# Wave 1 of a fused attention and MLP kernel: a third group of half-block products in place of four half-wave items, and another order of GpSimd's casts

## The chip, the cores and the metric

The kernel runs on one core of a Trainium2 chip. Its engines are TensorE (PE, with its weight loads shown as PEld), VectorE (DVE), ScalarE (ACT), GpSimd (POOL) and SyncE (SP, which issues most DMAs). Each engine works through its own instructions in the order of the program; semaphores hold an instruction until what it needs is there. The metric is the device time of one execution in microseconds (us).

## The reference

Linear attention with a decay for each head, block by block, and then an MLP on all 3072 tokens (4 batches of 768 positions, 8 heads of 64 make 512 columns; the hidden width is 2048):

```python
for b in range(nb):                       # blocks of 64 positions
    intra = np.einsum('bhic,bhjc->bhij', qb, kb) * Dmask[None]
    intra = np.einsum('bhij,bhjd->bhid', intra, vb)
    inter = np.einsum('bhid,bhde->bhie', qb * lam_pow[None], kv_state)
    out[:, :, sl] = intra + inter
    kv_state = lam_block[None, :, None, None] * kv_state + np.einsum('bhsd,bhse->bhde', kb * rev_pow[None], vb)
x = out.transpose(0, 2, 1, 3).reshape(B * S, H * D)
h = x @ w_in                              # 512 -> 2048
g = h * (1.0 / (1.0 + np.exp(-1.702 * h)))
return g @ w_out                          # 2048 -> 512
```

## The kernel before, in words

The tokens are worked in six waves of 512. Waves 0 and 1 take the first 256 positions of two batches each; waves 2 to 5 take 128 positions of all four batches. A wave is: load q, k and v (SP), scale and cast q and k to bf16 (`do_cast`, on GpSimd or VectorE), turn them so that the head dimension lies on the partitions (`turn_pe` on TensorE, or `turn_dma`, a transposing DMA that SP issues), attention, and the two products of the MLP. The attention of wave 1 goes by its two batches: `start(1, c)` makes the scores, which VectorE masks (`sm`, line 267), and `end(1, c)` multiplies them by v (`d_out`, line 316) and has ScalarE copy the result from PSUM into `xT`, the wave's x (line 221).

**Half-block products.** The MLP's products save an eighth of the multiplications by the seven-product scheme for 2 x 2 blocks. For the first product the two block rows are the two halves of the wave's tokens (256 each), the inner blocks the two halves of the 512 columns of x, and the two block columns are pairs of 128-wide blocks of the hidden width; four such blocks are a group (`GROUPS`). The factors of the seven products are blocks of x or the four sums `x_s` (`x_sums`, line 529, VectorE: s3, s1, s2 and s4 in that order, the last two depending on the one before), and blocks of `w_in` or sums of them (`in_sums`, line 520). In `in_product` (line 544 for the matmuls) each product is four matmuls of 128 x 256. Products 1 and 2 need only the first token half and no sum; 7 needs s3, 6 needs s2, 5 needs s1, 3 needs s4, and 4 needs the second token half. Products 1, 6, 5 and 3 pile up in one PSUM bank (X) one after the other, with a copy or an addition out of the bank after each; 2 has the bank Q, and 7 and 4 share V.

In the list of steps (`STEPS`, read by `one_step`) a small letter is the group's place and the digit the product: `a7v` is product 7 of the wave's first group, with `v` for "copied out by VectorE" (line 218), otherwise 1, 6 and 7 are copied out by ScalarE (line 221). The results of 2, 5 and 4 are added on VectorE to such a copy (`h_sb`, line 552). A capital letter is the GELU of a finished quarter on ScalarE (`A2`, line 563). `P10` is product 1 of the MLP's second product for the first 128 tokens of a half (line 461), `gl3` a sum of its factors (`g_s`, line 441, VectorE), where `l` and `h` are the lower and the upper half of the hidden width; `S0` to `S3` are the scores of the next wave (line 335), `M` and `m` their masks.

**Half-wave items.** `mlp1_half(w, c, fc)` computes two hidden blocks for one token half in the plain way: eight matmuls of 128 x 256 (line 414) into one bank and one GELU (line 416). Wave 1 has eight of them for hidden blocks 0 to 3 and 5 to 8, and seven-product groups only for the other eight blocks (`GR` gives group numbers for each wave).

**Order around the change.** All engines' work is written out by hand in program order (`manual_schedule`), and each engine keeps that order. Between `end(1, 0)` and the list for wave 1 the program has: a half-wave item, product 3 of wave 0 (`P31`), `start(1, 1)`, two items, `end(1, 1)`, an item, `x_sums(1)`, and four items of the second token half. GpSimd's casts of wave 2 stand among them in the order k, q, k, q (first half of the batches, then the second), each followed by its transposing DMA on SP. `gate_pool` is a one-element copy on GpSimd, used to make it wait until something is written; waves 2 to 5 have one behind `x_s` (step `G`).

Of the kernel before, what the change touches and what calls it, by code (L numbers as in the profile page):

```python
# [25 lines left out]
def kernel(  # L26
# [13 lines left out]
    nc = tc.nc  # L40
# [7 lines left out]
    G = W // P  # L48
# [14 lines left out]
    NW = S // P  # L63
# [9 lines left out]
    HF = 2  # L73
# [18 lines left out]
    def load(w, nms="kqv"):  # L92
        src = {"k": k, "q": q, "v": v}
        if w < ND:
            for c in range(HF):
                for nm in nms:
                    if w or c == 0 or nm != "v":
                        load_one(w, c, nm, src[nm])
        else:
            for nm in nms:  # L100
                for c in range(HF):
                    load_one(w, c, nm, src[nm])
# [140 lines left out]
    def turn_dma(w, c, nm):  # L243
        y = work.tile([P, 2 * NP, P], bf16, tag=f"{nm}T{c}", bufs={"k": 1, "q": 2}[nm], name=f"{nm}T")
        nc.sync.dma_start_transpose(out=y, in_=cast[w, c, nm].rearrange("p b c -> p (b c)"))
        trans[w, c, nm] = y
# [159 lines left out]
    def mlp1_half(w, c, fc):  # L406
        if w not in g_of:
            g_of[w] = gp.tile([P, FFC, W], bf16, tag="g", name="g_sb")
        cols = slice(c * W // 2, (c + 1) * W // 2)
        h = acc("ps_h", shape=[P, 2, W // 2], tag="mm")  # L410
        for u in range(2):
            j, i = w_in_of[fc + u]
            for kc in range(KC):
                nc.tensor.matmul(h[:, u, :], w_in_sb[j][:, kc, i * P : (i + 1) * P], xT[w][:, kc, cols],  # L414
                                 start=(kc == 0), stop=(kc == KC - 1))
        nc.scalar.activation(g_of[w][:, fc : fc + 2, cols], h, GELU)
# [13 lines left out]
    def token_half(w, i, kh):  # L430
        return g_of[w].rearrange("p (m two) (i t) -> p two i m t", two=2, i=2)[:, kh, i]
# [16 lines left out]
    def product(w, n, ts, ms=range(FFC // 2)):  # L448
        last = w == NW - 1
        key = ts[0] if last else 0  # L450
        if n == 1 and (last or ts[0] == 0) and ms[0] == 0:
            for c in "QVX":
                blocks[w, c, key] = acc(f"ps_{c}", shape=[P, 2, 256], tag="a" if last and ts[0] else "mm")
        bank = blocks[w, CHAIN[n], key]
        sums, raw = half_sum.get(w, [None] * 4), [[token_half(w, i, kh) for kh in range(2)] for i in range(2)]
        x = {1: raw[0][0], 2: raw[0][1], 4: raw[1][1], 5: sums[0], 6: sums[1], 7: sums[2], 3: sums[3]}[n]
        for t in ts:
            for m in ms:
                y = {1: (0, 0), 2: (1, 0), 3: (1, 1)}.get(n)
                y = w_half(m, *y) if y else TS[{4: 3, 5: 0, 6: 1, 7: 2}[n]][:, m]  # L460
                nc.tensor.matmul(bank[:, t], x[:, m, t * P : (t + 1) * P], y,  # L461
                                 start=(n in (1, 2, 7) and t == ts[0] * last and m == 0),
                                 stop=(m == FFC // 2 - 1), skip_group_check=True)
        if (last or ts[-1] == 1) and ms[-1] == FFC // 2 - 1:
            t = slice(ts[0], ts[0] + 1) if last else slice(0, 2)
            if n == 2 and w < NW - 1:
                c11[w] = partial(after_product, w, n, bank, t)
            else:
                after_product(w, n, bank, t)
# [24 lines left out]
                out=out.rearrange("(b s) d -> s b d", s=S)[w * P : (w + 1) * P, 2 * i + t.start : 2 * i + t.stop, cols],  # L494
                in_=o[:, t])

    GR = {w: (1, 2, 0, 3) if w > 1 else (0, 3) for w in range(1, NW)}
    TAGS = {w: ("aQXV", "mXVQ", "aQXV", "aXVQ") if w > 1 else ("aQXV", "aXVQ") for w in range(1, NW)}
    HALVES = (0, 2, 5, 7)
    GROUPS = (((4, 13), (14, 15)), ((0, 2), (1, 3)), ((6, 5), (8, 7)), ((10, 9), (12, 11)))  # L500
    USED = sorted({g for w in range(NW) for g in GR.get(w, ())})
    TI = {g: [const.tile([P, KC // 2, 2, P], bf16, name=f"w_in_t{g}{n}") for n in range(1, 5)] for g in USED}
# [22 lines left out]
    def x_sums(w):  # L525
        s1, s2, s3, s4 = x_sum[w] = [xp.tile([P, 2, 256], bf16, tag=f"xs{n}", bufs=1, name="x_s") for n in range(4)]
        a11, a12, a21, a22 = (x_half(w, i, kh) for i in range(2) for kh in range(2))
        for o, x, y, f in ((s3, a11, a21, SUB), (s1, a21, a22, ADD), (s2, s1, a11, SUB), (s4, a12, s2, SUB)):
            nc.vector.tensor_tensor(o, x, y, op=f)  # L529
# [35 lines left out]
    def one_step(w, s):  # L565
        if s[0] == "+":
            w, s = w + 1, s[1:]
        x, a = w + 1, s[1:]
        if s[0] == "f":
            mlp1(w, int(a))  # L570
        elif s[0] in "abcd":
            k = "abcd".index(s[0])
            in_product(w, GR[w][k], int(s[1]), TAGS[w][k], dve_copy if s[2:] == "v" else act_copy)
        elif s[0] in "ABCD":
            in_gelu(w, GR[w]["ABCD".index(s[0])], int(a))
        elif s[0] == "P":
            product(w, int(s[1]), (int(s[2]),))
        elif s[0] == "p":
            product(w, int(s[1]), (0, 1), {"a": range(4), "b": range(4, 6), "l": range(6), "h": range(6, 8)}[s[2]])
        elif s[0] == "W":  # L580
            weight_sums(int(a[0]), tuple(int(i) - 1 for i in a[1:]))
        elif s[0] == "I":
            in_sums(int(a))
        elif s[0] in "kq":
            do_cast(x, int(a), s[0], nc.vector)
        elif s[0] in "KQ":
            do_cast(x, int(a), s[0].lower(), nc.gpsimd)
        elif s[0] == "t":
            turn_dma(x, int(s[2]), s[1])
        elif s[0] == "v":  # L590
            cast_v(x, int(s[1]), ((act_copy, dve_copy)[s[2:] == "v"],))
        elif s[0] == "S":
            n_scores(x, int(a))
        elif s[0] == "M":
            n_masks(x, int(a))
        elif s[0] == "m":
            n_masks(x, int(a), True)
        elif s[0] == "R":
            n_rest(x)
        elif s[0] == "o":  # L600
            c11.pop(w)()
        elif s[0] == "X":
            x_sums(x)
        elif s[0] == "G":
            gate_pool(x_sum[w][3][0:1, 0, 0:1])
        elif s[0] == "g":
            m0, m1 = {"l": (0, 4), "h": (4, 8)}[s[1]]
            g_sums(w, m0, m1, tuple(int(c) - 1 for c in s[2:]))
        elif s[0] == "L":
            load(w + (1 if a == "w" else 2), "kq" if a == "k" else "v")  # L610
        else:
            raise ValueError(s)

    STEPS = {
# [24 lines left out]
    with tc.manual_schedule():  # L639
# [55 lines left out]
        def start(w, c):  # L695
            if c == 0:
                d_one(w, c)
                d_keep(w, c)
            for pp in range(2):
                d_scores(w, c, pp)  # L700
            d_even(w, c, ("mm", "a")[c])

        def end(w, c):
            oa, oz = d_out(w, c)
            t = acc("ps_kv", shape=[P, NP, D]) if w else states[w, c]
            if w == 0:
                nc.scalar.copy(seen, oz[:, 3, P - 1 : P])
            d_state(w, c, t, Z)
            if w == 0:
                d_inter(w, c, oz, 0, False)  # L710
            if w and c == 0:
                d_one(w, 1)
            d_x(w, c, 0, oa, act_copy)
            d_x(w, c, 1, oz, act_copy if w and c else dve_copy)
            if w:
                nc.vector.tensor_tensor(kv_sb[0][:, 2 * w + c], kept[w, c], t, op=ADD)
            else:
                nc.scalar.copy(kv_sb[0][:, 2 * w + c], t)
            if w and c == 0:
                d_keep(w, 1)  # L720

        def steps(w, names):
            for s in names.split():
                one_step(w, s)
# [23 lines left out]
        end(1, 0)  # L748
        steps(0, "P30 I2")
        turn_pe(1, 1, "q", act_copy)  # L750
        halves = [(c, fc) for c in range(HF) for fc in HALVES]
        for i, (c, fc) in enumerate(halves):
            if i == 1:
                steps(0, "P31")
                start(1, 1)
            if i == 3:
                end(1, 1)
            if i == 4:
                x_sums(1)
            mlp1_half(1, c, fc)  # L760
            if i in (1, 2, 3, 4):
                nm = "kq"[(i - 1) % 2]
                do_cast(2, (i - 1) // 2, nm, nc.gpsimd)
                turn_dma(2, (i - 1) // 2, nm)
            if i == 6:
                load(2, "v")
        steps(1, STEPS[1])
        for w in range(ND, NW):
            steps(w, STEPS[w])
# [30 lines left out]
```

## Time and profile before

| | |
|---|---|
| median of 3 runs | 192.86 us (192.72 to 193.34) |
| the profiled execution | 192.84 us; its span, first to last instruction, 191.1 us |
| PE busy | 184.6 us (97% of the span) |
| DVE busy | 156.3 us (82%) |
| ACT busy | 129.6 us (68%) |
| POOL busy | 53.7 us (28%) |
| TensorE clock granted | 1.00 |

The profile has one execution. In a timeline row the first number is the start of the first instruction, the second how long the merged instructions lasted, then engine, line, operation, the tile written and the tiles read, shapes, and in brackets how long the engine stood idle and what ended that. The start of a matmul is its issue; matmuls overlap, so a row of four 128 x 256 matmuls that lasts 0.60 us takes 0.44 us of the engine until the next row starts. In the chain of waits the rows are laid end to end.

### The profile page before, as it was taken

To read this page: it belongs to the slowest core of one execution; us is meant where nothing else is said; L and a number is where in the kernel's file an instruction comes from. 1 tells how busy PE (TensorE), PEld (TensorE's weight loads), DVE (VectorE), ACT (ScalarE), POOL (GpSimd) and SP (SyncE) were. 2 spreads that over 40 slices of the span, in tenths; PEclk is the share of its full clock that TensorE was granted. 3 is DMA by queue.
4 is the path that set the end of the run, shared out by engine and by line. 5 is a ranking of instruction groups with operands and counts; after the bars stand their busy time and mean duration, and the time that the engine had idled before them with its cause. 6 is when DMAs were issued, how large, how long until landed. Compare 5 with 4: busy or idle time off the path is not lost.

```text
span 191.1 us, 5544 instructions
## 1 busy us (share of the span) xinstructions
PE 184.6 (97%) x2297; PEld 152.2 (80%) x2297; DVE 156.3 (82%) x292; ACT 129.6 (68%) x242; POOL 53.7 (28%) x76
## 2 busy tenths in 40 slices
PE   7979999999999999999999999999999999999993
PEld 2557646888888888888888888888888888888882
DVE  1796699979978799879799879799789797888950
ACT  4948665257666986388896288885488876597611
POOL 5499000076495000195000294000492000000000
PEclk9999999999999999999999999999999999999999
DMA  4999999999997997868999555899565903300113
GB/s 144 313 290 197 204 200 209 321 310 229 215 241 178 214 247 165 207 163 139 208 243 216 187 153 127 197 241 230 175 152 122 209 4 113 110 3 0 54 59 110
DMA packets 89599, 33.91 MB, mean 177 GB/s; under 512 B 67430, under 2 KB 89446, under 8 KB 89574
## 3 DMA queue, kind: packets, MB, share of 16 engines
q1 hardware_dynamic: 84676, 28.84, 60.1%
q0 software_dynamic: 4896, 4.72, 14.5%
q8 instruction: 18, 0.29, 0.6%
q14 instruction: 7, 0.06, 0.1%
q10 hardware_dynamic: 2, 0.00, 0.0%
HBM read 27.26 MB, written 6.29 MB: 176 GB/s over the span
## 4 chain that ended last, share of the span: by engine, by line
PE 73%; DMA 11%; DVE 8%; POOL 2%; ACT 2%; issue 1%; SPq 0%; ACTq 0%
PE ps_X L461 19%; PE ps_hX L544 16%; PE ps_V L461 9%; PE ps_hV L544 8%; PE ps_Q L461 5%; DMA w_in<-in_moe_w_in_dram 5%; PE ps_hQ L544 4%; DVE w_in_t L520 3%; DMA kf<-in_k_dram 3%; DMA vf<-in_v_dram 3%; PE ps_h L414 2%; PE ps_s L335 2%; PE ps_o L390 2%; PE ps_fill L147 2%; POOL ks L202 1%; DVE sm L267 1%
## 5 line engine op out<-in xcount | busy, mean ns | idle before, releaser
L461 PEld LDWEIGHTS <-g_s 128*128 128x128 bf16 x384 | 37.0, 98 | 5.0
L563 ACT ACTIVATE g_sb<-h_sb 128x512 bf16<-128x512 f32 x54 | 32.6, 631 | 1.2 <-DVE h_sb L552 1.2
L544 PEld LDWEIGHTS <-w_in_t 128*128 128x128 bf16 x288 | 28.1, 98 | 3.4
L461 PEld LDWEIGHTS <-g_sb 128*128 128x128 bf16 x288 | 27.4, 98 | 4.1
L221 ACT COPY part<-ps_hX 128x512 f32<-128x512 f32 x32 | 18.3, 586 | 11.5 <-PE ps_hX L544 11.5
L461 PE MATMUL ps_X<-w_out_t,g_s 128*128 128x256 bf16 x192 | 23.1, 273 | 0.0
L544 PEld LDWEIGHTS <-w_in 128*128 128x128 bf16 x216 | 21.1, 98 | 2.5
L544 PE MATMUL ps_hX<-x_s,w_in_t 128*128 128x256 bf16 x144 | 21.6, 272 | 0.0
L441 DVE TENSOR_TENSOR g_s<-g_sb 128x1024 bf16<-128x1024 bf16 x24 | 16.3, 687 | 5.9 <-ACT g_sb L563 5.6
L634 POOL CAST behind_q<-x_s 1x1 f32<-1x1 bf16 x3 | 0.5, 174 | 60.3 <-DVE x_s L529 60.3
L209 POOL TENSOR_TENSOR qs<-qf,q_pow 128x512 bf16<-128x512 f32 x16 | 16.6, 1063 | 2.9 <-DMA qf<-in_q_dram 2.9
L209 POOL TENSOR_TENSOR ks<-kf,k_pow 128x512 bf16<-128x512 f32 x16 | 16.8, 1075 | 1.8 <-DMA kf<-in_k_dram 1.8
L474 ACT COPY part<-ps_X 128x512 f32<-128x512 f32 (+1 forms) x14 | 7.3, 522 | 13.0 <-PE ps_X L461 13.0
L218 DVE COPY part<-ps_hV 128x512 f32<-128x512 f32 x18 | 12.4, 688 | 3.7 <-PE ps_hV L544 3.7
L552 DVE TENSOR_TENSOR h_sb<-part,ps_hX 128x512 f32<-128x512 f32 x18 | 12.3, 681 | 2.7 <-PE ps_hX L544 2.7
L552 DVE TENSOR_TENSOR h_sb<-part,ps_hV 128x512 f32<-128x512 f32 x18 | 12.3, 684 | 1.0 <-PE ps_hV L544 1.0
L461 PE MATMUL ps_X<-w_out,g_sb 128*128 128x256 bf16 x96 | 12.6, 273 | 0.0
L461 PE MATMUL ps_Q<-w_out,g_sb 128*128 128x256 bf16 x96 | 12.5, 273 | 0.0
L552 DVE TENSOR_TENSOR h_sb<-part,ps_hQ 128x512 f32<-128x512 f32 x18 | 12.2, 679 | 0.0
L461 PE MATMUL ps_V<-w_out_t,g_sb 128*128 128x256 bf16 x96 | 12.0, 273 | 0.0
L563 ACT ACTIVATE g_sb<-ps_hX 128x512 bf16<-128x512 f32 x18 | 10.6, 588 | 1.8 <-PE ps_hX L544 1.8
L461 PE MATMUL ps_V<-w_out_t,g_s 128*128 128x256 bf16 x96 | 11.6, 273 | 0.0
(111 smaller groups left out, 362.3 us busy)
## 6 DMA issues: line engine op xcount, KB each, us to landing
kf<-in_k_dram SPq DMA_DIRECT2D x10, 512.0 KB, 6.4
qf<-in_q_dram SPq DMA_DIRECT2D x10, 512.0 KB, 7.2
vf<-in_v_dram SPq DMA_DIRECT2D x10, 512.0 KB, 6.0
out_dram<-o_sb SPq DMA_DIRECT2D x24, 128.0 KB, 2.4
out_dram<-o_sb SPq DMA_DIRECT2D x12, 256.0 KB, 2.7
w_out<-in_moe_w_out_dram POOLq DMA_DIRECT2D x4, 512.0 KB, 14.1
kf<-in_k_dram SPq DMA_DIRECT2D x4, 256.0 KB, 3.1
qf<-in_q_dram SPq DMA_DIRECT2D x4, 256.0 KB, 5.2
```

The lines of the kernel that those rows point to most:

```text
L147: nc.tensor.matmul(fill_ps[0], zero[:, 0:P], zero, start=True, stop=True)
L209: eng.tensor_tensor(x.rearrange("p b (r i j d) -> p j (b r) i d", i=2, j=2, d=D)[:, j], f.rearrange("p h (a d) -> p (h a) d", a=2).rearran ...
L218: nc.vector.tensor_copy(out, in_)
L221: nc.scalar.copy(out, in_)
L335: nc.tensor.matmul(s2[h][:, b, :], kT[hs, (b % 2) * NP + p, :], qT[hs, (b % 2) * NP + p, :], start=True, stop=True)
L441: nc.vector.tensor_tensor(o, x, y, op=f)
L461: nc.tensor.matmul(bank[:, t], x[:, m, t * P : (t + 1) * P], y, start=(n in (1, 2, 7) and t == ts[0] * last and m == 0), stop=(m == FFC // ...
L474: nc.scalar.copy(part[w, n, t.start][:, t], bank[:, t])
L520: nc.vector.tensor_tensor(o, x, y, op=SUB)
L544: nc.tensor.matmul(bank[:, u], z[:, kc], y[:, kc], start=(n in (1, 2, 7) and u + kc == 0), stop=(kc == 1), skip_group_check=True)
L552: nc.vector.tensor_tensor(h, h_part[w, g, {2: 1, 5: 7, 4: 6}[n]], bank, op=ADD)
L563: nc.scalar.activation(g_of[w][:, a : b + 1 : b - a, 256 * i : 256 * i + 256], bank, GELU)
```

## The change

Wave 1 gets a third group (blocks 0 to 3) computed by seven products, ahead of the other two, and four of the eight half-wave items go (blocks 0 to 3); the two items of the second token half move into the list of steps. GpSimd casts both k of wave 2, then waits for the last of the sums of x (`G`), then casts both q; the transposing DMAs on SP follow that order. The first group takes its banks from the pool of three (`mXVQ`), the other two from the pool of five.

```diff
-    GR = {w: (1, 2, 0, 3) if w > 1 else (0, 3) for w in range(1, NW)}
-    TAGS = {w: ("aQXV", "mXVQ", "aQXV", "aXVQ") if w > 1 else ("aQXV", "aXVQ") for w in range(1, NW)}
-    HALVES = (0, 2, 5, 7)
+    GR = {w: (1, 2, 0, 3) if w > 1 else (1, 0, 3) for w in range(1, NW)}
+    TAGS = {w: ("aQXV", "mXVQ", "aQXV", "aXVQ") if w > 1 else ("mXVQ", "aQXV", "aXVQ") for w in range(1, NW)}
+    HALVES = (5, 7)
...
+        elif s[0] == "h":
+            mlp1_half(w, 1, int(a))
...
     STEPS = {
-        1: ("a1 a7v a2 a6 b1 b7v A2 a5 b2 b6 B2 a4 a3 b5 b4 A5 P10 A4 b3 gl3 B4 B5 P11 gh3 S0 S1 M0 P20 m1 "
+        1: ("b2 a7v a6 b7v A2 a5 b6 a4 A5 a3 c1 A4 B2 b5 c7v c2 c6 B5 b3 b4 h5 C2 c5 B4 h7 c4 P10 c3 C5 P11 gl3 "
+            "C4 gh3 S0 S1 M0 P20 m1 "
             "Lk gl1 P70 P71 gl2 P21 v0 gh12 S2 S3 M2 m3 v1 o P40 P41 P60 gl4 gh4 P61 R P50 P51 +a1 X +a2 P30 "
             "P31 "),
...
-        halves = [(c, fc) for c in range(HF) for fc in HALVES]
-        for i, (c, fc) in enumerate(halves):
-            if i == 1:
-                steps(0, "P31")
-                start(1, 1)
-            if i == 3:
-                end(1, 1)
-            if i == 4:
-                x_sums(1)
-            mlp1_half(1, c, fc)
-            if i in (1, 2, 3, 4):
-                nm = "kq"[(i - 1) % 2]
-                do_cast(2, (i - 1) // 2, nm, nc.gpsimd)
-                turn_dma(2, (i - 1) // 2, nm)
-            if i == 6:
-                load(2, "v")
+        mlp1_half(1, 0, HALVES[0])
+        steps(0, "P31")
+        start(1, 1)
+        for c in range(HF):
+            do_cast(2, c, "k", nc.gpsimd)
+            turn_dma(2, c, "k")
+        mlp1_half(1, 0, HALVES[1])
+        steps(1, "a1 a2")
+        end(1, 1)
+        steps(1, "b1")
+        x_sums(1)
+        steps(1, "G")
+        for c in range(HF):
+            do_cast(2, c, "q", nc.gpsimd)
+            turn_dma(2, c, "q")
+        load(2, "v")
         steps(1, STEPS[1])
```

## The prediction

> **What bounds the kernel now.** I read the page first, for the engines' shares:
>
> ```profile
> PE 184.6 (97%) x2297; PEld 152.2 (80%) x2297; DVE 156.3 (82%) x292; ACT 129.6 (68%) x242; POOL 53.7 (28%) x76
> ```
>
> TensorE is busy nearly throughout, but a share over the span doesn't tell what happens in the stage that is changed. So next comes the chain of waits around wave 1:
>
> ```profile
> 47.52 2.80 DVE w_in_t L520 x3
> 50.32 2.41 DVE sm L267 x4
> ...
> 53.44 4.47 PE ps_h L414 x40
> 57.91 0.44 PE ps_hX L544 x4
> 58.35 0.44 PE ps_hV L544 x4
> ...
> 64.91 0.87 PE ps_X L461 x8
> 65.78 0.56 PE ps_s L335 x16
> ```
>
> Up to 52.7 VectorE carries it (sums of weights, then the four masks). From 53.44 to the end of the program it is TensorE without a hole: five half-wave items (40 matmuls), then the products. So whatever takes work off TensorE after 53.4 is worth just that work, and every wait that appears there is paid in full: no later idle time of TensorE can take it back. Third, VectorE's timeline, and GpSimd's beside it:
>
> ```profile
> 54.21 2.29 DVE L529 TENSOR_TENSOR x_s<-xT 128x512 bf16<-128x512 bf16 x2 [0.24 <-ACT xT L221]
> 56.54 1.15 DVE L529 TENSOR_TENSOR x_s<-x_s,xT 128x512 bf16<-128x512 bf16 x1
> 57.73 1.15 DVE L529 TENSOR_TENSOR x_s<-xT,x_s 128x512 bf16<-128x512 bf16 x1
> 58.83 0.69 DVE L218 COPY part<-ps_hV 128x512 f32<-128x512 f32 x1
> 59.43 0.68 DVE L552 TENSOR_TENSOR h_sb<-part,ps_hQ 128x512 f32<-128x512 f32 x1
> ...
> 66.10 0.69 DVE L441 TENSOR_TENSOR g_s<-g_sb 128x1024 bf16<-128x1024 bf16 x1 [0.72 <-ACT g_sb L563]
> ...
> 78.68 0.75 DVE L529 TENSOR_TENSOR x_s<-xT 128x512 bf16<-128x512 bf16 x2
> 79.47 0.42 DVE L529 TENSOR_TENSOR x_s<-x_s,xT 128x512 bf16<-128x512 bf16 x1
> 79.92 0.42 DVE L529 TENSOR_TENSOR x_s<-xT,x_s 128x512 bf16<-128x512 bf16 x1
> ```
>
> ```profile
> 52.99 2.05 POOL L209 TENSOR_TENSOR qs<-qf,q_pow 128x512 bf16<-128x512 f32 x2 [2.94 <-DMA qf<-in_q_dram]
> 55.00 2.42 POOL L209 TENSOR_TENSOR ks<-kf,k_pow 128x512 bf16<-128x512 f32 x2
> ```
>
> The reader should see three things. The four sums of x take 4.67 us in wave 1 (54.21 to 58.88), beside GpSimd's casts, and 1.66 us in wave 2 (78.68 to 80.34), where GpSimd stands still. In wave 1 that slowness is free, because TensorE's 40 matmuls, begun at 53.37, last until 57.75. And the sums can't begin before 54.2: ScalarE's copies of x release them.
>
> **The change, part by part.** All is summed against the profiled execution, 192.84 us (span 191.1 and 1.7 around it); the median of the runs is 192.86.
>
> TensorE's work: four items of eight matmuls (32) become seven products of four (28). A matmul of 128 x 256 takes 0.109 us (the 40), a product 0.436. Gain: 4 x 0.109 = 0.44 us, all on the path.
>
> Before 53.4: between the scores of `start(1, 1)` and `end(1, 1)` there stood two items, 16 matmuls; now an item, a1 and a2, also 16. The bank of a2 is the one that P31's result leaves at 50.22 (ScalarE's copy at 49.64, 0.58 long); a2's turn is at 51.53. So `end(1, 1)` and the copies of x stay where they are, the sums again start at 54.21, and the change is worth nothing here. The second k cast now follows the first: it needs a load issued at about 43.8 that takes 6.4 us (median of the page), so it runs from 50.2 to 52.3 or, at 1.23 us each, 52.7. It lies beside the masks at 50.25. Four masks beside GpSimd's casts at 43.07 took 2.48 us and 2.47 here without: nothing for it. And it is over before 54.21, so I take wave 2's pace for the sums: s3 ready at 54.63, s2 at 55.42, s4 at 55.87. That takes 3.0 us of work off VectorE, which was hidden.
>
> The cover is what goes. Behind `end(1, 1)` stood five items, 4.37 us, that need no sum; now only b1 and b2 stand there, until 54.25. Following TensorE's new order (b1, b2, a7, a6, b7, a5, b6, a4, a3), with three latencies: 0.05 us from a VectorE result to the matmul (mask ends 52.72, matmul 52.77); 0.64 us from a product's start to the start of the copy or addition that empties its bank (58.19 to 58.83); 0.60 us between VectorE's copies and additions in a row (58.83 to 59.43):
>
> a7 needs s3: 54.68 instead of 54.25, a wait of 0.43. a6 needs s2: 55.47 instead of 55.12, 0.35. a5 goes into the bank that ScalarE copies after a6: 55.47 + 0.64 + 0.58 + 0.05 = 56.74, and only b7 stands between (until 56.34): 0.40. In waves 2 to 5 two products stand there, just enough. Then b6 and a4 run until 58.05. a3 needs VectorE's addition of a5. After the sums VectorE has b2's addition at 55.80 (1.59 after the sums' start, as at 80.27 in wave 2), the copies of a7 and b7 at 56.40 and 57.00, and that addition at 57.60, ending at 58.28: a3 at 58.33, a wait of 0.28. Two chains, one over ScalarE (58.05) and one over VectorE (58.33), end near each other, so removing one alone would give little back. Sum of waits: 0.43 + 0.35 + 0.40 + 0.28 = 1.46 us.
>
> From a3 on, eleven products, two items and P10 (4.80 + 1.75 + 0.87 us) lead to P11 at 65.75; it was at 64.75 before. I find no wait in between: c6 comes at 60.5 and needs the copy of c1, done at 60.05 on ScalarE; b3 at 60.95 needs an addition done at 60.53; c5, c3 and both items have over half a microsecond.
>
> One more appears behind it. `C4`, a GELU, now stands behind ScalarE's copy of P11, and `gh3` needs it. The copy of P11 starts at 66.97 (P11's end plus 0.2, behind two GELUs 0.5 apart), C4 runs from 67.45 to 68.08, gh3 (0.69) ends at 68.80. P70's fifth matmul needs that; its turn is at 68.60 (P70 follows P11's start by 2.41, as 67.16 did 64.75). Wait: 0.25 us. Before, gh3 ended at 66.79, 0.8 us early. VectorE goes on with the masks at 68.71 instead of 66.71, 2.0 later, and TensorE is 1.25 later; the last masks of wave 2, which ended at 73.42, end at 75.4, and their matmuls, which began at 74.59, want them from 75.8 on. It has caught up when the next sums of x are due. I put nothing for it, and up to 0.3 if the masks slip.
>
> Added evictions: three additions and one copy on VectorE (4 x 0.68 = 2.7 us, less than the 3.0 that the sums give up), two copies of 0.59 on ScalarE, whose 9.9 busy of 12.9 us hold them. They cost nothing apart from the waits named. GpSimd's gate (0.17 us) holds the two q casts until 56.1; behind it on GpSimd there is nothing else before wave 3. Four casts of 1.05 end at 60.3. SP's queue has k's second transposing DMA at 58.0 and q's at 59.4 and 60.7, as it had four at 56.2 to 60.7 before; the load of v behind them stays at 62.0. The last lands near 63.5; S0 wants it at 66.7. Hidden with 3 us to spare, and beyond that each microsecond would cost one.
>
> Sum: -0.44 + 1.46 + 0.25 = +1.27 us, 194.1 us.
>
> **The rivals.** *TensorE is fed in time.* If sums, copies and additions are done when their products' turn comes, only the work counts: 192.84 - 0.44 = 192.4. It speaks for this that VectorE gets 3.0 us back and is idle for 18% of the span. It is decided by a5's addition: a3's turn without waits is 53.37 + 8 x 0.436 = 56.9, so the addition has to end by then, and for no loss by 57.3; I have it at 58.28, and the ScalarE chain alone at 58.05. Chance 0.09.
>
> *The sums stay slow.* Should k's second load land over 1.5 us later, its cast lies beside the sums again. At the rows of wave 1 (4.67 instead of 1.66 us) a3 moves by 3.0 us: 197.1. Against it: the load was issued in the same place, and GpSimd waits for nothing else. Chance 0.05. [...]
>
> *The clock falls.* Four holes in four microseconds might lower the granted clock. Priced at half speed for the eight products after a3, 8 x 0.436 = 3.5 us: 197.6. Against it stands this row of the waits, a hole twice as long as any here, with the granted clock at 1.00 throughout:
>
> ```profile
> PE ps_t L238 <- DVE qs L202: 0.9, 1, 0.9
> ```
>
> Chance 0.02. [...]
>
> **How the numbers follow.** The forecast has 0.82; 0.02 is for what I haven't seen. Its own range: without the wait at P70 and with latencies 0.1 us shorter at the five waits, 193.3; with the sums at their mean of 0.57 us (0.6 more) and another 0.3 for the masks, 195.0. These ends hold about 0.8 of all cases, so they are the range. What can be told from no change is about 0.3%, 0.58 us. Faster by more than that can't come from 0.44 us: 0.02. The same: the first rival and the forecast's low tail, 0.12. Slower: 0.86.
>
> **What would show it.** Right: sums of x near 0.42 us each; TensorE idle before a7, a6, a5 and a3 by 0.3 to 0.4 us each; P11 at about 65.8 and the scores at 66.7; the fifth matmul of P70 waiting for a `g_s` row near 68.8; no other hole behind. Wrong: x_s rows above 1 us, a6 and a3 following without a hole, or a P11 before 65.0.

## The result, and the profile after

The changed kernel takes 194.38 us (median of 20 runs), the kernel before, measured beside it, 193.03 us (median of 20). The ratio, which here as in every experiment leaves out runs more than 1.5% above the fastest of their kernel, is 1.0062, with a 95% interval of 1.0039 to 1.0086. The kernel is slower by 1.2 us, about twice what can be told from no change. The profiled execution took 193.97 us with a span of 192.3 us, 1.13 us more than before. Its trace has no record of the clock, but its 128 x 256 matmuls are issued 0.109 us apart wherever nothing holds them, as before.

The page's line of the engines says next to nothing of it:

```profile
PE 185.4 (96%) x2293; PEld 152.0 (79%) x2293; DVE 154.7 (80%) x296; ACT 130.4 (68%) x244; POOL 53.8 (28%) x77
```

TensorE has four matmuls fewer and 0.8 us more busy time. Half of that lies ahead of the changed stage (50.5 us up to the end of wave 1's attention, 50.1 before). The other half is a matter of reading: a matmul that ends a burst is shown at its full 0.27 us, though the next could follow after 0.109, and five holes bring that five times. What happened stands in the timeline of wave 1 (start, length, engine, line, operation, tiles; in brackets the idle time and its releaser; "..." where rows are left out, among them all weight loads):

```profile
54.08 0.76 DVE L529 TENSOR_TENSOR x_s<-xT 128x512 bf16<-128x512 bf16 x2 [0.31 <-ACT xT L221]
54.55 0.60 PE L544 MATMUL ps_hV<-x_s,w_in_t 128*128 128x256 bf16 x4 [0.27 <-DVE x_s L529]
54.87 0.42 DVE L529 TENSOR_TENSOR x_s<-x_s,xT 128x512 bf16<-128x512 bf16 x1
55.33 0.42 DVE L529 TENSOR_TENSOR x_s<-xT,x_s 128x512 bf16<-128x512 bf16 x1
55.35 0.61 PE L544 MATMUL ps_hX<-x_s,w_in_t 128*128 128x256 bf16 x4 [0.20 <-DVE x_s L529]
55.67 0.68 DVE L552 TENSOR_TENSOR h_sb<-part,ps_hQ 128x512 f32<-128x512 f32 x1
...
56.00 0.59 ACT L221 COPY part<-ps_hX 128x512 f32<-128x512 f32 x1 [1.47 <-PE ps_hX L544]
...
56.27 1.28 DVE L218 COPY part<-ps_hV 128x512 f32<-128x512 f32 x2
...
56.64 1.03 PE L544 MATMUL ps_hX<-x_s,w_in_t 128*128 128x256 bf16 x8 [0.24 <-ACT part L221]
57.47 0.68 DVE L552 TENSOR_TENSOR h_sb<-part,ps_hX 128x512 f32<-128x512 f32 x1
...
58.20 0.60 PE L544 MATMUL ps_hX<-x_s,w_in 128*128 128x256 bf16 x4
...
66.84 0.58 ACT L474 COPY part<-ps_X 128x512 f32<-128x512 f32 x1
...
67.30 0.64 ACT L563 ACTIVATE g_sb<-h_sb 128x512 bf16<-128x512 f32 x1
...
67.98 0.69 DVE L441 TENSOR_TENSOR g_s<-g_sb 128x1024 bf16<-128x1024 bf16 x1 [2.17 <-ACT g_sb L563]
68.03 2.18 PE L461 MATMUL ps_V<-w_out_t,g_s 128*128 128x256 bf16 x16
```

The four sums run at 0.42 us, from 54.08 to 55.75. The matmul rows show a7 at 54.55, a6 at 55.35, a5 at 56.64 and a3 at 58.20, three of them with a releaser in brackets: twice a sum, once ScalarE's copy. The brackets (0.27, 0.20, 0.24) are smaller than what is lost, because a matmul's modelled end lies beyond the issue of the next. The loss is read from issue to issue, less the 0.109 us that a matmul takes of the engine: 0.435 us ahead of a7, 0.366 ahead of a6, 0.400 ahead of a5, 0.256 ahead of a3. The fifth hole hides inside a row: the 16 matmuls of the last line last 2.18 us where they lasted 1.91 before. Its fifth is issued at 68.73, just behind `gh3` (67.98 + 0.69), 0.26 us late. This is the row of before:

```profile
67.16 1.91 PE L461 MATMUL ps_V<-w_out_t,g_s 128*128 128x256 bf16 x16
```

The chain of waits, which was TensorE alone from 53.44 on, now leaves it twice, for ScalarE's copies of x, the sums and VectorE's copies up to a3, and for ScalarE's last steps ahead of `gh3`:

```profile
52.97 1.08 ACT xT L221 x2
54.05 0.02 issue
54.08 0.77 DVE x_s L529 x2
54.85 0.02 issue
54.87 0.43 DVE x_s L529
...
55.67 0.68 DVE h_sb L552
56.35 0.93 DVE part L218 x2
57.28 0.19 issue
57.47 0.69 DVE h_sb L552
58.16 0.04 issue
58.20 1.47 PE ps_hX L544 x12
...
66.84 0.58 ACT part L474
67.41 0.54 ACT g_sb L563
67.95 0.03 issue
67.98 0.70 DVE g_s L441
```

Two distances sum it up, and they serve for the experiments too. From the first matmul of the MLP behind `end(1, 1)` (called the entry from here on) to the first score `S0` it took 12.35 us before (53.37 to 65.72) and takes 13.35 now (53.24 to 66.59): +1.00. From `S0` to the end it took 125.42 and takes 125.68: +0.26. The entry itself was 0.13 us earlier.

### The profile page after: what moved, and what is told of

Its sections match the earlier page's. It is cut to its first block, busy times and chain, and to the rows that moved or that the text cites. A ratio compares the mean times of both kernels' runs of the same rounds, so it can differ in the third digit from the quotient of the medians.

```text
span 192.3 us, 5546 instructions
## 1 busy us (share of the span) xinstructions
PE 185.4 (96%) x2293; PEld 152.0 (79%) x2293; DVE 154.7 (80%) x296; ACT 130.4 (68%) x244; POOL 53.8 (28%) x77
## 4 chain that ended last, share of the span: by engine, by line
PE 89%; DVE 6%; ACT 2%; issue 1%; ACTq 0%; DVEq 0%
PE ps_X L461 21%; PE ps_hX L544 16%; PE ps_V L461 11%; PE ps_hV L544 8%; PE ps_h L402 5%; PE ps_Q L461 5%; PE ps_hQ L544 4%; PE ps_h L414 4%; DVE sm L267 3%; PE ps_t L238 2%; PE ps_o L390 2%; PE ps_s L335 2%; PE ps_fill L147 2%; PE ps_s L259 1%; PE ps_o L377 1%; PE ps_o L316 1%
## 5 line engine op out<-in xcount | busy, mean ns | idle before, releaser
L563 ACT ACTIVATE g_sb<-h_sb 128x512 bf16<-128x512 f32 x57 | 34.5, 631 | 1.2 <-DVE h_sb L552 1.2
L544 PEld LDWEIGHTS <-w_in_t 128*128 128x128 bf16 x304 | 29.6, 98 | 4.8 <-issue 0.9
L221 ACT COPY part<-ps_hX 128x512 f32<-128x512 f32 x34 | 19.6, 587 | 12.3 <-PE ps_hX L544 12.3
L544 PEld LDWEIGHTS <-w_in 128*128 128x128 bf16 x228 | 22.2, 98 | 2.9 <-issue 0.3
L544 PE MATMUL ps_hX<-x_s,w_in_t 128*128 128x256 bf16 x152 | 22.6, 272 | 0.4 <-ACT part L221 0.2
L552 DVE TENSOR_TENSOR h_sb<-part,ps_hX 128x512 f32<-128x512 f32 x19 | 12.9, 681 | 4.1 <-PE ps_hX L544 4.1
L218 DVE COPY part<-ps_hV 128x512 f32<-128x512 f32 x19 | 13.0, 687 | 3.2 <-PE ps_hV L544 3.2
L552 DVE TENSOR_TENSOR h_sb<-part,ps_hV 128x512 f32<-128x512 f32 x19 | 13.0, 685 | 1.8 <-PE ps_hV L544 1.8
L552 DVE TENSOR_TENSOR h_sb<-part,ps_hQ 128x512 f32<-128x512 f32 x19 | 12.9, 680 | 0.0
L563 ACT ACTIVATE g_sb<-ps_hX 128x512 bf16<-128x512 f32 x19 | 11.2, 590 | 2.4 <-PE ps_hX L544 2.4
```

The source lines that it names most:

```text
L218: nc.vector.tensor_copy(out, in_)
L221: nc.scalar.copy(out, in_)
L544: nc.tensor.matmul(bank[:, u], z[:, kc], y[:, kc], start=(n in (1, 2, 7) and u + kc == 0), stop=(kc == 1), skip_group_check=True)
L552: nc.vector.tensor_tensor(h, h_part[w, g, {2: 1, 5: 7, 4: 6}[n]], bank, op=ADD)
L563: nc.scalar.activation(g_of[w][:, a : b + 1 : b - a, 256 * i : 256 * i + 256], bank, GELU)
```

## Experiments

Three theories are named in the expectations. "Cover": the half-wave items that filled TensorE while the sums and copies were made are gone, and nothing later gives the time back. "Casts": holding q back behind the gate costs. "Load": VectorE and ScalarE got too many evictions.

**1. Only the new order of the casts.** The kernel before, with both k cast first, then the gate, then both q; products and items unchanged.

```diff
+                for kc in range(HF):
+                    do_cast(2, kc, "k", nc.gpsimd)
+                    turn_dma(2, kc, "k")
...
+                steps(1, "G")
+                for qc in range(HF):
+                    do_cast(2, qc, "q", nc.gpsimd)
+                    turn_dma(2, qc, "q")
...
-            if i in (1, 2, 3, 4):
-                nm = "kq"[(i - 1) % 2]
-                do_cast(2, (i - 1) // 2, nm, nc.gpsimd)
-                turn_dma(2, (i - 1) // 2, nm)
```

> The kernel before with only the casts of the change: k, k behind the second scores of wave 1, the gate behind the sums of x, then q, q. Theory 'cover' (the time is lost in five waits of TensorE, because the sums and evictions lost the half-wave items that stood before them): the sums of x take 1.7 us instead of 4.7, but 40 matmuls hide them either way, so no change in time, within 0.15 us of before, span near 191.1. Rival 'casts' (holding q back until the sums are done is what costs): 0.8 to 1.3 us slower, with the scores of wave 2 waiting for the transposes of q. Rival 'load' (VectorE and ScalarE can't carry the added evictions): no change, as nothing is added here.

Measured: a ratio of 0.9991 (0.9963 to 1.0019). The sums take 0.42 us each and end at 55.76, and TensorE has no use for them until 58.04:

```profile
53.23 4.54 PE L414 MATMUL ps_h<-xT,w_in 128*128 128x256 bf16 x40
57.61 0.60 PE L544 MATMUL ps_hX<-xT,w_in 128*128 128x256 bf16 x4
58.04 0.60 PE L544 MATMUL ps_hV<-x_s,w_in_t 128*128 128x256 bf16 x4
```

Entry to `S0`: 12.34 us, as before. The casts alone cost nothing and bring nothing. "Casts" falls, and sums that are 3 us quicker are worth nothing behind 40 matmuls of cover.

**2. The change without the gate.** All four casts as soon as their data are there; everything else as changed.

```diff
-        steps(1, "G")
```

> The changed kernel without the gate: GpSimd goes on to the casts of q when they have landed (near 52.9), so they run beside the sums of x. Theory 'cover': the sums take 4.7 us instead of 1.7 (1.15 to 1.26 each), a7, a6 and a3 start later with them, and a3 stands near 61.0 instead of 58.2: 2.5 to 3.0 us slower than the changed kernel, about 197. Rival 'casts': without the gate the time falls back towards before, 193. Rival 'load': slower by what the sums take more, like 'cover'. [...]

Measured: 197.24 us, a ratio of 1.0228 (1.0186 to 1.0270). The last three sums run beside the casts of q, and a6 waits for one of them:

```profile
52.77 4.65 POOL L209 TENSOR_TENSOR qs<-qf,q_pow 128x512 bf16<-128x512 f32 x4 [0.63 <-PE ps_o L298]
...
53.72 1.61 DVE L529 TENSOR_TENSOR x_s<-xT 128x512 bf16<-128x512 bf16 x2 [0.31 <-ACT xT L221]
55.37 1.15 DVE L529 TENSOR_TENSOR x_s<-x_s,xT 128x512 bf16<-128x512 bf16 x1
56.55 1.15 DVE L529 TENSOR_TENSOR x_s<-xT,x_s 128x512 bf16<-128x512 bf16 x1
...
56.58 0.61 PE L544 MATMUL ps_hX<-x_s,w_in_t 128*128 128x256 bf16 x4 [1.78 <-DVE x_s L529]
```

The hole ahead of a6 grew from 0.37 to 1.94 us. Entry to `S0` took 16.08 us, 2.73 more than in the changed kernel. The wider hole is 1.58 of that. The rest is in the table of stretches (start and end, length, busy time of the engines with their instructions, granted clock, DMA share, GB/s):

```profile
53.95:57.36 3.41, 1.38 (x12) 0.99 (x12) 3.34 (x4) 0.36 (x2) 3.41 (x3) 1.00 0.81 197
57.36:60.77 3.41, 3.30 (x17) 2.14 (x15) 2.90 (x6) 1.99 (x4) 0.06 (x1) 0.50 1.15 150
60.77:64.18 3.41, 3.41 (x34) 3.04 (x32) 2.42 (x4) 3.02 (x7) 0.00 (x0) 1.00 0.82 182
```

In the middle stretch the clock is 0.50 and matmuls are issued 0.213 us apart instead of 0.109. Fourteen of them lose 1.40 us together, less the hole at a3 (0.26) that disappears behind them: 1.15, just what was left. So that the 2.5 to 3.0 us that I had expected came out is luck: I had them from the sums alone, and these gave 1.58. Still the gate is what makes the new order bearable: without the cover, slow sums that were free before cost 2.7 us, 1.15 of it through the clock.

**3. The cover put back, with the same work.** The same products and items, but the two items that remain stand where the waits are, and `c1` stands ahead of `a3`. (The GELUs `C2` and `B5` change places with it.)

```diff
-        1: ("b2 a7v a6 b7v A2 a5 b6 a4 A5 a3 c1 A4 B2 b5 c7v c2 c6 B5 b3 b4 h5 C2 c5 B4 h7 c4 P10 c3 C5 P11 gl3 "
+        1: ("b2 h5 a7v a6 b7v A2 h7 a5 b6 a4 A5 c1 a3 A4 B2 b5 c7v c2 c6 C2 b3 b4 B5 c5 B4 c4 P10 c3 C5 P11 gl3 "
```

> The changed kernel with the same work in another order in wave 1: the two items of the second token half move forward, h5 behind b2 and h7 between b7 and a5, c1 goes ahead of a3, and the GELU C2 ahead of B5; the place of C4 is left. Theory 'cover': the waits at a7 (0.43), a6 (0.37), a5 (0.40) and a3 (0.26) go, 1.46 in all; the one at the fifth matmul of P70 (0.26) stays. P11 starts near 64.2, span near 190.8, 1.3 to 1.5 us faster than the changed kernel and 0.2 to 0.4 faster than before. Rival 'load': the evictions are as many and in the same stretch, so most of the time stays: 0 to 0.4 us faster than the changed kernel, with new holes at c5, c3 or P10. Rival 'casts': no change from the changed kernel.

Measured: 192.70 us, a ratio of 1.0004 (0.9977 to 1.0031). All four holes are gone: entry to `S0` takes 11.90 us, 1.45 less than in the changed kernel and 0.45 less than before. That is the sum of the four waits and the four matmuls. The hole in `P70` stays (0.26 us; `S0` to the end 125.70). VectorE and ScalarE have all the added evictions here, so "load" falls as well. The first group takes its banks from the pool of three here too, so that part of the change cost nothing either. The runs are too few to show the 0.2 to 0.4 us that I expected against the kernel before; the trace has 0.45 up to `S0` and gives 0.28 of it back behind it.

**4. The same, with `C4` ahead of `C5`.** ScalarE then does the GELU that `gh3` needs before its copy of `P11`.

```diff
-... c4 P10 c3 C5 P11 gl3 " "C4 gh3 ...
+... c4 P10 C4 c3 P11 gl3 " "C5 gh3 ...
```

> As the kernel before this one, and the GELU C4 changes place with C5, so that it no longer stands behind the copy of P11. Theory 'cover': the wait at P70 goes too, 0.25 us more: span near 190.55, about 0.5 to 0.6 us (0.3%) faster than before, which is the 0.44 us of matmuls and 0.1 of an earlier start. Rival 'load': gh3 waits for something else instead, VectorE being behind, and the wait at P70 stays within 0.1 us. Rival 'casts': as the changed kernel.

Measured: 192.09 us, a ratio of 0.9965 (0.9944 to 0.9986): faster than both kernels. TensorE's timeline from the entry:

```profile
53.05 0.61 PE L544 MATMUL ps_hX<-xT,w_in 128*128 128x256 bf16 x4
53.49 0.60 PE L544 MATMUL ps_hQ<-xT,w_in 128*128 128x256 bf16 x4
53.93 1.04 PE L414 MATMUL ps_h<-xT,w_in 128*128 128x256 bf16 x8
54.80 0.60 PE L544 MATMUL ps_hV<-x_s,w_in_t 128*128 128x256 bf16 x4
...
66.38 1.91 PE L461 MATMUL ps_V<-w_out_t,g_s 128*128 128x256 bf16 x16
```

No row has a bracket, and the 16 matmuls of the last row are back at 1.91 us. Entry to `S0` takes 11.90 us and `S0` to the end 125.41: together 0.46 us less than before, about the 0.44 that four matmuls are worth.

**5. One of two chains shortened.** The changed kernel with a7 copied out by ScalarE instead of VectorE.

```diff
-        1: ("b2 a7v a6 ...
+        1: ("b2 a7 a6 ...
```

> The changed kernel with the copy out of a7 on ScalarE instead of VectorE. It takes one copy of 0.6 us out of VectorE's chain to a3 and puts one of 0.58 us ahead of a6's copy on ScalarE. Theory 'cover', with its claim that two chains end near each other: a7's copy lies on ScalarE at about 55.2 to 55.8, a6's copy at 56.0 as before, a5 stays at 56.64, a5's addition comes as soon as VectorE has b7's copy behind it, and a3 has its natural turn at 57.95 behind a4. The hole at a3 (0.26 us) goes to under 0.1, the other three holes of 0.37 to 0.44 us stay, and the whole gains at most 0.2 us on the changed kernel: a ratio of 1.004 to 1.006. Rival 'load' (VectorE got too many evictions, and they set the pace): one of 0.6 us fewer gives back about 0.6 us, a ratio of 1.002 or less.

Measured: 194.1 us, a ratio of 1.0078 (1.0041 to 1.0115), not to be told from the changed kernel's. Entry to `S0` takes 13.24 us, 0.11 less. The hole at a3 is 0.14 us, where "cover" said under 0.1: I had let a3 follow a4, but it still waits for the addition of a5, which now waits for a5 itself:

```profile
57.73 0.69 DVE L552 TENSOR_TENSOR h_sb<-part,ps_hX 128x512 f32<-128x512 f32 x1 [0.21 <-PE ps_hX L544]
```

From a5's start (57.02) to a3's (58.47) it is 1.45 us, and the two products between and a5 itself fill 1.31. Giving VectorE 0.6 us back is worth 0.1, since the chain over ScalarE, which sets a5's start, ends next to it: its end is a5's addition and not, as I had it, a4.

**6 and 7. Later sums.** The changed kernel with two or five more additions on VectorE ahead of wave 1's sums. They write what the last sum overwrites.

```diff
+        for _ in range(2 if w == 1 else 0):      # 5 in the other kernel
+            nc.vector.tensor_tensor(s4, a11, a21, op=SUB)
```

> The changed kernel with two more additions of VectorE (each 0.42 us, over the same operands as the last sum, written over later, so the result is unchanged) ahead of wave 1's four sums of x: the sums start 0.84 us later. Theory 'cover' (nothing is left behind the end of wave 1's attention to hide a late sum, and no later idle time of TensorE gives it back): the hole ahead of a7 grows from 0.44 to about 1.25 us, those behind it stay as they are, and the span grows by 0.8 us over the changed kernel: about 195.2, a ratio of 1.010 to the kernel before; the clock stays 1.00. Rival (TensorE's loss is set by the evictions and not by the sums): the holes at a5 and a3 shrink as the one at a7 grows, and less than 0.4 us is lost.

Measured: 194.51 us, a ratio of 1.0095 (1.0051 to 1.0139). The hole ahead of a7 is 1.23 us, 0.80 more than in the changed kernel; the other holes are as they were (0.35, 0.40, 0.25); entry to `S0` takes 14.14 us, 0.79 more:

```profile
54.46 0.61 PE L546 MATMUL ps_hV<-x_s,w_in_t 128*128 128x256 bf16 x4 [1.07 <-DVE x_s L531]
```

(The two added lines move line 544 to 546 here.) The ratios alone, 1.0095 against 1.0062, have intervals that overlap, so it is the trace that shows the 0.8 us. Its span was only 192.2 us because this execution entered the wave 0.90 us earlier (52.34).

> The same with five such additions: the sums start 2.1 us later. Theory 'cover' at a clock that stays 1.00: a hole of about 2.5 us ahead of a7, 2.1 us more than the changed kernel, about 196.5, a ratio of 1.017. It also asks what lowered the clock in the kernel without the gate, where the longest hole was 1.94 us and TensorE was busy for 1.38 of 3.41 us before the clock was at 0.5 for 3.4 us: if it is the low share of busy time in such a stretch, it falls here too, for about 3.4 us, and up to 1.7 us more are lost (198.2, ratio up to 1.026); if it is the number of holes or their being near each other, it stays at 1.00.

Measured: 196.98 us, a ratio of 1.0227 (1.0158 to 1.0296). The hole ahead of a7 is 2.62 us, 2.18 more, but entry to `S0` takes 16.55 us, 3.20 more. The clock fell again:

```profile
54.28:57.69 3.41, 0.96 (x8) 0.62 (x9) 3.20 (x10) 0.07 (x1) 0.00 (x0) 1.00 0.89 228
57.69:61.11 3.42, 3.42 (x19) 2.41 (x17) 2.63 (x5) 1.55 (x3) 3.30 (x5) 0.50 1.19 93
```

The missing 1.02 us are the matmuls of the slow stretch, most of which lose 0.104 us each (1.67 in all), less the holes at a5 and a3 (0.66) that vanish there. Up to the point where the clock falls, every wait of a sum is paid in full.

## Why the prediction was right

It gave 194.1 us and a sum of +1.27 on the profiled execution. The profile has +1.13 and the medians 1.2 us (0.8 to 1.7 by the interval).

- *TensorE's work, −0.44.* Shown by experiment 4: with no wait left, entry to `S0` is 0.45 us shorter than before.
- *The four waits, 0.43 + 0.35 + 0.40 + 0.28 = 1.46.* Measured 0.435, 0.366, 0.400 and 0.256, 1.46 in all. Experiment 3 removes them by order alone and gets 1.45 back; experiments 6 and 7 make the first of them longer, and the later sums are paid in full. The three latencies, read from rows of before, carried over to a place that the trace of before didn't have.
- *P70's fifth matmul, 0.25.* Measured 0.26; experiments 3 and 4 differ by it. Behind it nothing more slipped: `S0` to the end grew by 0.26, so the masks of wave 2 cost nothing, the lower of the two ends given.
- *The sums at wave 2's pace.* 0.42 us each, from 54.08. Experiment 2 is the rival "the sums stay slow" come true, for another reason than a late load. I priced it at 3.0 us from wave 1's rows. The wait itself cost 1.58, because the first sum slipped in at 0.42, and the fourth, slow too, was done at 57.70, long before a3 wanted it (60.37). The clock cost another 1.15. Beside the casts the last three sums took 1.27, 1.15 and 1.15 us, where each takes 0.42 without them.
- *The added evictions and the casts at nothing.* Experiments 1 and 3 bear it out. The load of v was issued at 62.66, 0.7 us later than I had it, and stayed hidden.
- *"Removing one alone would give little back."* Experiment 5: 0.11 us of 0.26. The chain over ScalarE was a little longer than the 58.05 I gave it, since I ended it with a4 and left out a5's addition.
- *The entry "stays where it is".* This is the 0.14 us between 1.27 and 1.13. The third sum of weights ahead of the masks took 0.42 us instead of 1.27, as the k that GpSimd casts beside it landed 0.3 us later (cast from 48.10 instead of 47.78; this sum starts at 47.97, before at 47.87), and the entry came 0.13 us earlier. Over the nine profiled executions the entry lies between 52.34 and 53.62, so I take it for an arrival that varies and no part of the change.
- *"The clock falls", chance 0.02.* In the profiled execution of the changed kernel no two matmuls of a product in wave 1 are issued 0.21 us apart, as they are where experiment 2 has a clock of 0.50 (0.213). Three of its twenty runs have a mean clock of 0.991, though, which is what one stretch of 3.41 us at half clock would take off (an estimate: 3.41 x 0.5 / 193); four of the 48 runs of the kernel before that stand beside the experiments have 0.982 to 0.991. Where the clock fell in those no trace shows, so it is not shown that the holes of the change did it. The reason I gave was too weak in any case: one hole of 1 us at full clock doesn't tell what several holes do. Experiment 6 added 0.80 us of idle time and its profile has a clock of 1.00 from 51.80 to 59.47; experiment 2 added 1.58, its clock was 0.50 for 3.41 us, and all six of its runs have a mean clock of 0.980 to 0.991.

## What to carry to other kernels

When an engine runs without a hole to the end of the program, price a change there as the work removed plus each new wait in full. Build the wait from latencies that the trace shows elsewhere in the same kernel; here that gave five terms to within 0.03 us. Work that needs nothing from the critical chain covers a wait only where the wait is: the same two items and `c1`, moved by a few places, gave back 1.45 us. With `C4` ahead of `C5` as well, +1.2 us against the kernel before became −0.7 (interval −1.1 to −0.3).

## What the runs showed of the hardware

In wave 1 of two profiled executions the granted clock was 0.50 for about 3.4 us, behind holes of 1.94 and 2.62 us. In experiment 2 TensorE was busy for 1.38 of the 3.41 us from 53.95 to 57.36 (40%), with the hole of 1.94 us in them, and the clock was 0.50 from 57.36 to 60.77. In experiment 7, with a hole of 2.62 us, it was busy for 0.96 of the 3.41 us from 54.28 to 57.69 (28%), and the clock was 0.50 from 57.69 to 61.11. In experiment 6, with a hole of 1.23 us, it was busy for 2.20 of the 3.41 us from 51.80 to 55.21 (65%), and the clock was 1.00 there and in the 3.42 us behind.

At the end of the kernel before, where TensorE runs out of work, it was busy for 1.54 of the 3.42 us from 186.38 to 189.80 (45%, columns as in experiment 2), and the clock is 1.00 there and up to the last instruction:

```profile
186.38:189.80 3.42, 1.54 (x15) 1.13 (x12) 0.25 (x1) 0.74 (x2) 0.00 (x0) 1.00 0.44 154
189.80:191.14 1.34, 0.00 (x0) 0.00 (x0) 0.00 (x0) 0.00 (x0) 0.00 (x0) 1.00 0.00 0
```

All these shares rest on the modelled ends of the matmuls, and each is of one execution. The profiled executions of experiments 1 and 3, without a hole from the entry to `S0`, have a mean clock of 0.998; where in them it was lower is not shown. The fall in experiment 7 speaks against the number of holes as the cause, since experiment 6 has as many, at a clock of 1.00. Whether the busy share or the length of the hole counts, and from what value on, these executions don't show. How the place of a hole bears on what it costs stays open too: no run varied that.
